# Fourteen rounding casts of a fused attention and mixture-of-experts kernel go from ScalarE to DMAs that GpSimd issues; five copies go from VectorE to ScalarE

## The chip, the cores and the metric

The kernel runs on one core of a Trainium2 chip. The metric is the device time of one execution in microseconds (us); the time shown for a kernel is the median of several runs. A profile is one further execution, recorded by the hardware profiler.

## What is computed

The reference has two parts. The first is an attention with random features, for 4 batches, 8 heads, 576 positions and 64 columns, with 128 features:

```python
def phi(x):
    proj = np.einsum('bhsd,md->bhsm', x, omega)
    sq = np.sum(x * x, axis=-1, keepdims=True) / 2.0
    h = proj - sq
    h = h - np.max(h, axis=-1, keepdims=True)
    return np.exp(h) / np.sqrt(m)
q_p, k_p = (phi(q_s), phi(k_s))
kv = np.einsum('bhsm,bhsd->bhmd', k_p, v)
z = np.sum(k_p, axis=2)
num = np.einsum('bhsm,bhmd->bhsd', q_p, kv)
den = np.einsum('bhsm,bhm->bhs', q_p, z)[..., None] + 1e-06
```

The quotient num/den is a table of 2304 tokens by 512 columns. The second part sends every token through 8 experts with weights w1 (512 by 1024) and w2 (1024 by 512), weighted by a gate matrix that is normalised 8 times over rows and columns:

```python
for e in range(E):
    h = np.maximum(x @ w1[e], 0.0)
    ye = h @ w2[e]
    out += P[:, e:e + 1] * ye
```

## The kernel before, in words

All matrix products of the experts run in float32r, a rounded form of float32. An operand is therefore split into a rounded high part (a copy with a change of type, a "cast") and a low part (operand minus high part, a "low"), and a product is made of three matmuls. On top of that the products are done by a Strassen-like scheme with seven products, numbered 1 to 7; their operands are quarters of a matrix, or sums of quarters.

Tokens come in 4 chunks of 576. A chunk's operands are made while the attention of the next tokens still runs: for chunk 0 the generator `token_operands` makes the sums on GpSimd, the casts on ScalarE (`cast`, line 120) and the lows on VectorE (line 125), and SyncE then writes each operand to DRAM. In the same way `first_splits` makes the seven operands of the first unit's w1: sums on GpSimd (line 308), casts on ScalarE (line 312), lows on VectorE (line 316). The text below calls these "token cast 2", "token low 2", "weight cast 2", "weight low 2" and so on, by the number of the product.

The attention is a software pipeline of 36 jobs (a half head group of keys or queries each). `tick(j)` issues one turn of it: projections of job j, the transposes of job j+2, the transposed copy `th` of those (line 448 on ScalarE for keys, line 450 on VectorE for queries), row maxima and shifts (lines 470 to 477, VectorE), exponentials (lines 486 and 490, ScalarE), key-value products or numerators and quotients. The sums of squares of a later job (line 415 on ScalarE, then a tree of five halving additions and two small instructions on GpSimd, lines 419 to 421) are issued near the start of a turn. I call the seven GpSimd instructions a "square set".

Twice in each turn `go_on()` takes one step of the generators above. Their steps are strings, c for a cast, l for a low, s for a sum, with one step at each bar or blank:

```python
plan = "|c1 |c3 l1.s5|c2 l3|c5 l2.s7| l5.s6|c7 |c6 l7| l6.s4| |c4 | l4|"
...
for step in "|s5.c1 | l1|c2 |c5 l2| l5.s6.s7| |c4 |c6 l4|c7 l6.s3| l7| |c3 | l3|".split():
```

So each low is issued three steps, or one and a half turns, behind its cast. Within the attention every engine executes its instructions in the order in which they were written (the list `pinned`).

Queries, keys and values come in by DMAs of SyncE; before the change GpSimd issues no DMA. After the attention, units of expert products follow until the end (lines 727 and 833, TensorE).

Of the kernel before, what the change touches and what calls it, by code (L numbers as in the profile page):

```python
# [16 lines left out]
def raw(ap):  # L17

    return ap.bitcast(F32)
# [3 lines left out]
def moe_attention_kernel(  # L23
# [23 lines left out]
    nc = tc.nc  # L47
# [51 lines left out]
    def token_tile():  # L99
        return xs.tile([P, 2, 2, HL], F32R, tag="xs", bufs=XSB, name="xs")  # L100

    def token_operands(c, x):

        def q(r, h):
            h = 1 - h
            return x[:, 2 * r : 2 * r + 2, h * HL : (h + 1) * HL]

        last = c == NCH - 1
        gate_steps = logits(c, x)
        if last:  # L110
            next(gate_steps)

        def total(o, i, s):
            eng = nc.vector if last else nc.gpsimd
            a, b = {5: (q(0, 1), s), 6: (q(1, 1), s), 7: (q(1, 1), q(0, 1)), 4: (q(1, 0), s)}[i]
            eng.tensor_tensor(o, a, b, op=ALU.subtract)

        def cast(i, o):
            t = token_tile()
            nc.scalar.copy(t[:, 0], o)  # L120
            return t

        def low(i, o, t):
            eng = nc.gpsimd if c == 1 and i in (2, 5, 7) else nc.vector
            eng.tensor_tensor(t[:, 1], o, raw(t[:, 0]), op=ALU.subtract)  # L125
            xdram[c, i] = xd.tile([P, 2, 2, HL], F32, name=f"xd{c}_{i}")
            nc.sync.dma_start(out=xdram[c, i], in_=raw(t))

        if last:
            sums = [  # L130
                sc.tile([P, H * 2 * D], F32, tag="sq", bufs=2, name="sx")[:, : 2 * HL].rearrange("p (k t) -> p k t", k=2)
                for _ in range(2)
            ]
            at = {1: q(0, 0), 5: sums[0], 6: sums[1], 3: q(1, 1), 7: q(0, 1), 2: q(1, 0), 4: sums[0]}
            tiles = {}
            for step in "c1.s5.c5.l1 s6.c6.l5 c3.l6 s7.l3.c7 l7.c2 s4.l2.c4 l4".split():
                n = len(traced)
                for what in step.split("."):
                    i = int(what[1])
                    if what[0] == "s":  # L140
                        total(at[i], i, {5: q(0, 0), 6: sums[0], 4: sums[1]}.get(i))
                    elif what[0] == "c":
                        tiles[i] = cast(i, at[i])
                    else:
                        low(i, at[i], tiles[i])
                        xop[0, c, i] = tiles[i]
                        j = i
                if j in (3, 2):
                    load_next()
                pinned.extend(traced[n:])  # L150
                first(0, c, j, 0)
                first(0, c, j, 1)
                next(gate_steps, None)
                yield
            return


        if c == 0:
            at = {i: {3: q(1, 1), 7: q(0, 1), 2: q(1, 0)}.get(i, q(0, 0)) for i in ORDER}
            plan = "|c1 |c3 l1.s5|c2 l3|c5 l2.s7| l5.s6|c7 |c6 l7| l6.s4| |c4 | l4|"  # L160
        else:
            at = {1: q(0, 0), 3: q(1, 1), 2: q(1, 0)}
            for n, i in enumerate((5, 6, 7, 4)):
                at[i] = vts[n].rearrange("p h c -> p (h c)")[:, : 2 * HL].rearrange("p (k t) -> p k t", k=2)
            plan = "|s5.c1.c3 s7.l1|s6.c2 l3.l2|w.w.c5 c7|w.l5.s4 l7.w|c6 c4|l6 l4"
        tiles = {}
        for n, step in enumerate(plan.split()):
            for part in step.split("|"):
                for what in part.split(".") if part else ():
                    if what == "w":  # L170
                        next(w2_sums)
                        continue
                    i = int(what[1])
                    if what[0] == "s":
                        total(at[i], i, {5: q(0, 0), 6: at[5], 4: at[6]}.get(i))
                    elif what[0] == "c":
                        tiles[i] = cast(i, at[i])
                    else:
                        low(i, at[i], tiles.pop(i))
                yield  # L180
            next(gate_steps, None)


    def logits(c, x):


        nt = CT // 2
        lgs = []
        for h in range(2):
            lp = bank("lp")  # L190
            for k in range(KD):
                nc.tensor.matmul(
                    lp[k * GC : (k + 1) * GC, :HL], lhsT=wgs[:, k, :], rhs=x[:, k, h * HL : (h + 1) * HL],
                    start=True, stop=True,
                )
            lg = sc.tile([P, HL], F32, tag="lg", bufs=2, name="lg")
            nc.scalar.copy(lg, lp[:, :HL])
            lgs.append(lg)
        yield
        for h, lg in enumerate(lgs):  # L200
            gp = bank("gp")
            for j in range(nt):
                nc.tensor.transpose(gp[:, j * P : (j + 1) * P], lg[:, j * P : (j + 1) * P], ident)
            t0 = c * CT + h * nt
            nc.vector.tensor_reduce(
                prob[:, t0 : t0 + nt, :],
                gp[:, : nt * P].rearrange("p (t a e) -> p t e a", a=KD, e=GC)[:, :, :E, :],
                axis=AX.X, op=ALU.add,
            )
# [81 lines left out]
    def first_splits():  # L291

        def q(r, h):
            return wst[0, 1, r][:, :, 1 - h]

        tmp[0] = wp.tile([P, 2, HD], F32, tag="t", bufs=1, name="t")
        at = {1: q(0, 0), 7: q(0, 1), 2: q(1, 0), 4: q(1, 1), 5: tmp[0], 6: tmp[0], 3: tmp[0]}
        sums = {
            5: (q(0, 1), q(1, 1), ALU.add), 6: (tmp[0], q(0, 0), ALU.subtract),
            3: (q(1, 0), tmp[0], ALU.subtract), 7: (q(0, 0), q(0, 1), ALU.subtract),  # L300
        }
        for step in "|s5.c1 | l1|c2 |c5 l2| l5.s6.s7| |c4 |c6 l4|c7 l6.s3| l7| |c3 | l3|".split():
            for part in step.split("|"):
                for what in part.split(".") if part else ():
                    i = int(what[1])
                    if what[0] == "s":
                        a, b, op = sums[i]
                        nc.gpsimd.tensor_tensor(at[i], a, b, op=op)
                    elif what[0] == "c":
                        hi = wp.tile([P, 2, HD], F32R, tag="w1h", bufs=7, name="wh")  # L310
                        lo = wp.tile([P, 2, HD], F32R, tag="w1l", bufs=7, name="wl")
                        nc.scalar.copy(hi, at[i])
                        wt[0, 1, i] = (hi, lo)
                    else:
                        hi, lo = wt[0, 1, i]
                        nc.vector.tensor_tensor(lo, at[i], raw(hi), op=ALU.subtract)
                yield
# [125 lines left out]
    def transposed_copy(jb):  # L443

        which, tp = jb[0], tps.pop(jb)
        th = sc.tile([P, 4, P], F32, tag="th", bufs=2, name="th")
        if which == "k":
            nc.scalar.copy(th.rearrange("p a s -> p (a s)"), tp)
        else:
            nc.vector.tensor_copy(th.rearrange("p a s -> p (a s)"), tp)  # L450
        ths[jb] = th
# [229 lines left out]
    def load_next():  # L681

        while loads:
            u, c, i = loads.pop(0)
            if i in RES:
                if (c, i) not in xres:
                    xres[c, i] = op_.tile([P, 2, 2, HL], F32R, name=f"xr{c}_{i}")
                    nc.sync.dma_start(out=raw(xres[c, i]), in_=xdram[c, i])
                xop[u, c, i] = xres[c, i]
                continue  # L690
            if len(early) < 2:
                xop[u, c, i] = oa[0].tile([P, 2, 2, HL], F32R, tag="oa", bufs=2, name="oa")
                early.append(i)
            else:
                xop[u, c, i] = token_tile()
            nc.sync.dma_start(out=raw(xop[u, c, i]), in_=xdram[c, i])
            return
# [237 lines left out]
    jobs = []  # L935
# [4 lines left out]
    def q_of(b):  # L940
        return [("q", (b, i // 2), i % 2, 4 * b + i // 2 * 2) for i in range(4)]
# [16 lines left out]
    jobs += mix(k_of(3), q_of(2))  # L958
    jobs += q_of(3) + [qr(0), qr(1)]

    need, seen = [], set()
    for i, jb in enumerate(jobs):
        for w in ("k", "v") if jb[0] == "k" else ("q",):
# [136 lines left out]
    xt, i, t = turned.pop(0)  # L1100
# [4 lines left out]
    xt, i, t = turned.pop(0)  # L1105
# [45 lines left out]
    for s, (u, n) in enumerate(steps):  # L1151
        c = n // (CT // 2)
# [79 lines left out]
```

## Time and profile before

| what | value |
|---|---|
| median of 3 runs | 1578.07 us (1577.44 to 1579.23) |
| the profiled execution | 1577.75 us, span 1576.0 us |
| TensorE (PE), matmuls | 1562.6 us, 99% of the span |
| VectorE (DVE) | 1363.5 us, 87% |
| ScalarE (ACT) | 766.5 us, 49% |
| GpSimd (POOL) | 277.7 us, 18% |
| the attention | from 0 to about 153 us; the experts behind it |

The span is the time from the first to the last instruction in the profile; the execution's own time is 1.75 us longer. Shares are over the whole span, and the attention, where the changed instructions stand, has other shares than the experts. TensorE's granted clock is full in every slice.

### The profile page before, as it was taken

The page shows a single profiled execution, that of the slowest core. Times are in us where ns is not written, and L with a number is a line of the kernel's source. Part 1 is how long each engine was busy: PE and PEld are TensorE (multiplying, and loading weights), DVE is VectorE, ACT ScalarE, POOL GpSimd, SP SyncE. Part 2 cuts the span into 40 slices and gives each one's busy share as a digit, 9 for nine tenths or more (in the row PEclk, how much of TensorE's full clock was granted, in tenths as well). Part 3 has the DMA queues.
Part 4 walks back from the last instruction along what each step waited for, and adds up shares of the span by engine and source line. Part 5 has one row for each costly group of instructions (what it writes and reads, how often), then busy time and mean ns, then how long its engine had stood idle before and what let it go on. Part 6 is the DMA issues. An engine that isn't in the chain of part 4 may idle for free.

```text
span 1576.0 us, 31251 instructions
## 1 busy us (share of the span) xinstructions
PE 1562.6 (99%) x12295; PEld 1537.0 (98%) x12295; DVE 1363.5 (87%) x2573; ACT 766.5 (49%) x1387; POOL 277.7 (18%) x285
## 2 busy tenths in 40 slices
PE   9999999999999999999999999999999999999999
PEld 8887999999999999999999999999999999999998
DVE  6999899989889898889888888989888888888776
ACT  8998654444444443444444444444343444444342
POOL 6665211111011111112010111111010111110000
PEclk9999999999999999999999999999999999999999
DMA  9646876656666666656566666656566655656572
GB/s 222 144 149 254 329 253 216 214 186 212 223 209 215 222 209 214 220 185 224 202 217 210 217 217 208 224 183 222 201 226 219 218 201 212 228 173 215 185 229 88
DMA packets 105730, 330.81 MB, mean 210 GB/s; under 512 B 14704, under 2 KB 43888, under 8 KB 105584
## 3 DMA queue, kind: packets, MB, share of 16 engines
q1 hardware_dynamic: 105296, 328.55, 61.8%
q8 instruction: 98, 1.61, 0.4%
q14 instruction: 48, 0.39, 0.1%
q10 hardware_dynamic: 288, 0.26, 0.0%
HBM read 307.54 MB, written 21.23 MB: 209 GB/s over the span
## 4 chain that ended last, share of the span: by engine, by line
PE 92%; DVE 5%; ACT 2%; DMA 1%; issue 0%; POOL 0%; DVEq 0%; SPq 0%; ACTq 0%; POOLq 0%
PE hx L727 25%; PE x L833 24%; PE z L833 19%; PE hz L727 19%; PE pp L460 2%; PE p L914 1%; DVE sqs L470 1%; PE kv L497 1%; PE tp L440 1%; PE np L581 1%; DMA xd<-xs 1%; DMA xs<-xd 1%; DVE xs L125 1%; PE qp L557 1%; DVE wl L267 0%
## 5 line engine op out<-in xcount | busy, mean ns | idle before, releaser
L727 PE MATMUL hx<-xs,wh 128*128 128x384 f32 x1528 | 367.1, 335 | 0.8 <-ACT hr L756 0.6
L727 PE MATMUL hz<-xs,wh 128*128 128x384 f32 x1144 | 282.5, 336 | 0.9 <-DMA xs<-xd 0.4
L727 PEld LDWEIGHTS hx<-xs,wh 128*128 128x128 f32 x1528 | 265.4, 188 | 2.1 <-ACT hr L756 0.9
L233 POOL TENSOR_TENSOR st<-st 128x512 f32<-128x512 f32 x75 | 117.3, 1564 | 620.7 <-DVE wl L267 616.3
L814 ACT ACTIVATE bh<-hr 128x512 fp32r<-128x512 f32 x141 | 89.2, 633 | 243.2 <-PE x L833 237.6
L864 DVE SCALAR_TENSOR_TENSOR out<-x,prob,out 128x256 f32<-128x256 f32 x324 | 153.9, 478 | 57.2 <-PE x L833 55.4
L727 PEld LDWEIGHTS hz<-xs,wh 128*128 128x128 f32 x1144 | 199.9, 188 | 1.8 <-DVE bl L776 0.7
L727 PE MATMUL hx<-xs,wl 128*128 128x384 f32 x764 | 199.7, 335 | 0.0
L811 DVE TENSOR_TENSOR sl<-sm,sh 128x512 fp32r<-128x512 f32 x141 | 114.5, 812 | 43.5 <-ACT sh L810 36.8
L727 PE MATMUL hz<-xs,wl 128*128 128x384 f32 x572 | 151.8, 335 | 0.0
L266 ACT CAST wh<-st 128x512 fp32r<-128x512 f32 x172 | 103.3, 620 | 99.0 <-PE hx L727 50.8
L727 PEld LDWEIGHTS hx<-xs,wl 128*128 128x128 f32 x764 | 137.3, 188 | 0.0
L810 ACT CAST sh<-sm 128x512 fp32r<-128x512 f32 x141 | 87.6, 621 | 101.7 <-PE z L833 83.0
L267 DVE TENSOR_TENSOR wl<-st,wh 128x512 fp32r<-128x512 f32 x172 | 124.0, 731 | 8.9 <-ACT wh L266 8.8
L776 DVE SCALAR_TENSOR_TENSOR sm<-hr,sm 128x256 f32<-128x256 f32 x282 | 126.5, 449 | 3.1
L797 ACT CAST sh<-sm 128x512 fp32r<-128x512 f32 x140 | 87.1, 622 | 67.7 <-PE x L833 65.5
L833 PE MATMUL z<-wh,sh 128*128 128x256 f32 x564 | 116.6, 281 | 2.1 <-ACT sh L793 1.3
L833 PE MATMUL x<-wl,sh 128*128 128x256 f32 x564 | 114.9, 280 | 0.0
L833 PE MATMUL z<-wl,sh 128*128 128x256 f32 x564 | 114.5, 280 | 0.0
L833 PE MATMUL x<-wh,sl 128*128 128x256 f32 x564 | 114.0, 279 | 0.0
L784 ACT ACTIVATE ah<-hr 128x256 fp32r<-128x256 f32 x141 | 59.0, 418 | 111.9 <-PE x L833 99.7
L833 PE MATMUL x<-wh,sh 128*128 128x256 f32 x564 | 112.8, 280 | 0.0
(192 smaller groups left out, 3556.1 us busy)
## 6 DMA issues: line engine op xcount, KB each, us to landing
xs<-xd SPq DMA_DIRECT2D x327, 768.0 KB, 4.5
st<-in_moe_w_dram SPq DMA_DIRECT2D x66, 512.0 KB, 4.8
xd<-xs SPq DMA_DIRECT2D x21, 768.0 KB, 5.3
v<-in_v_dram SPq DMA_DIRECT2D x8, 512.0 KB, 6.9
q<-in_q_dram SPq DMA_DIRECT2D x8, 512.0 KB, 7.2
k<-in_k_dram SPq DMA_DIRECT2D x7, 512.0 KB, 7.2
out_dram<-out SPq DMA_DIRECT2D x18, 128.0 KB, 4.3
oa<-xd SPq DMA_DIRECT2D x2, 768.0 KB, 8.8
```

The source lines that it names most:

```text
L233: nc.gpsimd.tensor_tensor(o, a, b, op=op)
L266: nc.scalar.copy(hi, o)
L267: nc.vector.tensor_tensor(lo, o, raw(hi), op=ALU.subtract)
L727: nc.tensor.matmul(pb, lhsT=a[:, k, g * P : (g + 1) * P], rhs=x[:, b, k, :], start=i in (1, 5, 2) and j == 0, stop=j == len(prods) - 1, sk ...
L776: nc.vector.scalar_tensor_tensor(o, in0=a, scalar=0.0, in1=b, op0=ALU.max, op1=op)
L784: nc.scalar.activation(ah, a11, AF.Relu)
L797: nc.scalar.copy(sh, sm)
L810: nc.scalar.copy(sh, sm)
L811: nc.vector.tensor_tensor(sl, sm, raw(sh), op=ALU.subtract)
L814: nc.scalar.activation(bh, a[:, 1:], AF.Relu)
L833: nc.tensor.matmul(pb, lhsT=ops[s][i][a][:, f], rhs=wt[u, 2, i][b][:, f], start=bool(start) and j == 0, stop=j == len(prods) - 1, skip_gro ...
L864: nc.vector.scalar_tensor_tensor(o, in0=pb, scalar=p, in1=o, op0=ALU.mult, op1=ALU.add)
```

## The change

The casts of chunk 0's seven token operands and of the seven operands of the first w1 are no longer ScalarE instructions. Each is a DMA from SBUF to SBUF that GpSimd issues, with a change of type on the way: 128 by 768 elements (384 KB) for a token cast, 128 by 512 (256 KB) for a weight cast. And of the queries' transposed copies, five (jobs 14, 18, 23, 27 and 30, issued in turns 12, 16, 21, 25 and 28) go from VectorE to ScalarE.

```diff
         def cast(i, o):
             t = token_tile()
-            nc.scalar.copy(t[:, 0], o)
+            if c == 0:
+                nc.gpsimd.dma_start(out=t[:, 0], in_=o)
+            else:
+                nc.scalar.copy(t[:, 0], o)
             return t
...
                         lo = wp.tile([P, 2, HD], F32R, tag="w1l", bufs=7, name="wl")
-                        nc.scalar.copy(hi, at[i])
+                        nc.gpsimd.dma_start(out=hi, in_=at[i])
                         wt[0, 1, i] = (hi, lo)
...
-        if which == "k":
+        if which == "k" or jb in on_scalar:
             nc.scalar.copy(th.rearrange("p a s -> p (a s)"), tp)
...
+    on_scalar = [jb for jb in jobs[13:32] if jb[0] == "q"][::2]
```

The change moves instructions on three engines. The first place is GpSimd around weight casts 2 and 5, about 55 to 66 us in the trace. The rows are the end of a square set (`sq`, `sqs`) and the two sums 6 and 7 of the weight operands (`t`, `st`); brackets name the semaphores that an instruction waits for. Before:

```order
L419 TENSOR_TENSOR sq<-sq 128x16x4 [waits Pool_49]
L419 TENSOR_TENSOR sq<-sq 128x16x2 [waits Pool_49]
L420 TENSOR_TENSOR sqs<-sq 128x16 [waits DVE_49,Pool_49]
L421 TENSOR_SCALAR sqs<-sqs 128x16 [waits Pool_49]
L308 TENSOR_TENSOR t<-t,st 128x512 [waits DVE_49]
L308 TENSOR_TENSOR st<-st 128x2x256
```

After, with the line numbers of the changed kernel (3 higher here):

```order
L422 TENSOR_TENSOR sq<-sq 128x16x2 [waits Pool_49]
L423 TENSOR_TENSOR sqs<-sq 128x16 [waits DVE_49,Pool_49]
L424 TENSOR_SCALAR sqs<-sqs 128x16 [waits Pool_49]
L315 DMA wh<-st 128x2x256
L315 DMA wh<-t 128x512
L311 TENSOR_TENSOR t<-t,st 128x512 [waits DMASW2_49,DVE_49]
L311 TENSOR_TENSOR st<-st 128x2x256
```

Both weight casts now stand on GpSimd behind the square set, and the sum behind them waits for a DMA too. On VectorE weight low 2 stands where it stood, but waits for the DMA of GpSimd in place of ScalarE. Before:

```order
L477 TENSOR_TENSOR ex<-pp,cn 128x512 [waits DVE_49]
L316 TENSOR_TENSOR wl<-st,wh 128x512 [waits DMAHW3_49,Activation_49]
L470 TENSOR_REDUCE sqs<-pp 128x4 [waits PE_49] x2
L475 TENSOR_REDUCE cn<-sqs 128x8 [waits DVE_49]
L477 TENSOR_TENSOR ex<-pp,cn 128x512 [waits DVE_49]
L450 COPY th<-tp 128x512 [waits PE_49]
```

After:

```order
L480 TENSOR_TENSOR ex<-pp,cn 128x512 [waits DVE_49]
L319 TENSOR_TENSOR wl<-st,wh 128x512 [waits DMAHW3_49,DMASW1_49]
L473 TENSOR_REDUCE sqs<-pp 128x4 [waits PE_49] x2
L478 TENSOR_REDUCE cn<-sqs 128x8 [waits DVE_49]
L480 TENSOR_TENSOR ex<-pp,cn 128x512 [waits DVE_49,Activation_49]
```

The row maxima of the next turn stand right behind the low, and the copy `th` of that turn is gone from VectorE.

The second place is GpSimd around weight casts 4, 6 and 7, about 70 to 79 us in the trace, from the end of one square set over the next to weight sum 3. Before:

```order
L421 TENSOR_SCALAR sqs<-sqs 128x16 [waits Pool_49]
L419 TENSOR_TENSOR sq<-sq 128x16x32 [waits Activation_49]
L419 TENSOR_TENSOR sq<-sq 128x16x16 [waits Pool_49]
L419 TENSOR_TENSOR sq<-sq 128x16x8 [waits Pool_49]
L419 TENSOR_TENSOR sq<-sq 128x16x4 [waits Pool_49]
L419 TENSOR_TENSOR sq<-sq 128x16x2 [waits Pool_49]
L420 TENSOR_TENSOR sqs<-sq 128x16 [waits Pool_49]
L421 TENSOR_SCALAR sqs<-sqs 128x16 [waits Pool_49]
L308 TENSOR_TENSOR t<-st,t 128x512 [waits DVE_49]
```

After:

```order
L424 TENSOR_SCALAR sqs<-sqs 128x16 [waits Pool_49]
L315 DMA wh<-st 128x2x256
L422 TENSOR_TENSOR sq<-sq 128x16x32 [waits Activation_49]
L422 TENSOR_TENSOR sq<-sq 128x16x16 [waits Pool_49]
L422 TENSOR_TENSOR sq<-sq 128x16x8 [waits Pool_49]
L422 TENSOR_TENSOR sq<-sq 128x16x4 [waits Pool_49]
L422 TENSOR_TENSOR sq<-sq 128x16x2 [waits Pool_49]
L423 TENSOR_TENSOR sqs<-sq 128x16 [waits Pool_49]
L424 TENSOR_SCALAR sqs<-sqs 128x16 [waits Pool_49]
L315 DMA wh<-t 128x512
L315 DMA wh<-st 128x2x256
L311 TENSOR_TENSOR t<-st,t 128x512 [waits DMASW4_49,DVE_49]
```

Weight cast 4 stands behind the first square set, casts 6 and 7 behind the second.

The third place is GpSimd from token sum 5 to token sum 7 (`xf`), about 90 to 99 us in the trace. Before:

```order
L116 TENSOR_TENSOR xf<-xf 128x2x384 [waits DVE_49,PE_49]
L419 TENSOR_TENSOR sq<-sq 128x16x32 [waits Activation_49]
L419 TENSOR_TENSOR sq<-sq 128x16x16 [waits Pool_49]
L419 TENSOR_TENSOR sq<-sq 128x16x8 [waits Pool_49]
L419 TENSOR_TENSOR sq<-sq 128x16x4 [waits Pool_49]
L419 TENSOR_TENSOR sq<-sq 128x16x2 [waits Pool_49]
L420 TENSOR_TENSOR sqs<-sq 128x16 [waits Pool_49]
L421 TENSOR_SCALAR sqs<-sqs 128x16 [waits Pool_49]
L116 TENSOR_TENSOR xf<-xf 128x2x384
```

After, where `xs` is a token operand:

```order
L116 TENSOR_TENSOR xf<-xf 128x2x384 [waits DMASW6_49,DVE_49,PE_49]
L121 DMA xs<-xf 128x2x384 [waits DMASW0_49]
L422 TENSOR_TENSOR sq<-sq 128x16x32 [waits Activation_49]
L422 TENSOR_TENSOR sq<-sq 128x16x16 [waits Pool_49]
L422 TENSOR_TENSOR sq<-sq 128x16x8 [waits Pool_49]
L422 TENSOR_TENSOR sq<-sq 128x16x4 [waits Pool_49]
L422 TENSOR_TENSOR sq<-sq 128x16x2 [waits Pool_49]
L423 TENSOR_TENSOR sqs<-sq 128x16 [waits Pool_49]
L424 TENSOR_SCALAR sqs<-sqs 128x16 [waits Pool_49]
L315 DMA wh<-t 128x512 [waits DMASW1_49]
L121 DMA xs<-xf 128x2x384
L116 TENSOR_TENSOR xf<-xf 128x2x384
```

Token cast 2 stands ahead of the square set, weight cast 3 and token cast 5 behind it. The order of the instructions on TensorE and on SyncE is the same before and after.

## Rows read from the trace of the kernel before

**Rows 1.** The chain of work that ended last: start us, us, engine, tile, line.

```profile
65.07 1.07 ACT qt L564 x2
...
70.18 0.51 ACT wh L312
...
79.23 0.72 ACT xs L120
...
85.67 0.33 DVE prob L205 x2
...
90.49 0.60 DVE th L450
...
125.45 0.69 PE np L581 x16
```

**Rows 2.** Busy time in a stretch (us): PE, PEld, DVE, ACT, POOL, clock, DMA, GB/s.

```profile
60.00:80.00 20.00, 19.76 (x336) 17.66 (x338) 18.06 (x43) 19.20 (x47) 13.83 (x24) 1.00 0.06 15
```

**Rows 3.** GpSimd's timeline, 50 to 75 us: start us, us, instruction, idle time before it.

```profile
51.22 3.68 POOL L419 TENSOR_TENSOR sq<-sq 128x512 f32<-128x512 f32 x5 [4.88 <-ACT sq L415]
...
55.51 3.34 POOL L419 TENSOR_TENSOR sq<-sq 128x512 f32<-128x512 f32 x5
...
59.24 0.64 POOL L421 TENSOR_SCALAR sqs<-sqs 128x16 f32<-128x16 f32 x1
...
64.37 1.27 POOL L308 TENSOR_TENSOR t<-t,st 128x512 f32<-128x512 f32 x1 [4.49 <-DVE wl L316]
...
69.70 3.35 POOL L419 TENSOR_TENSOR sq<-sq 128x512 f32<-128x512 f32 x5
...
74.02 3.38 POOL L419 TENSOR_TENSOR sq<-sq 128x512 f32<-128x512 f32 x5
```

**Rows 4.** VectorE's timeline: weight lows 1, 2, 5, 4 and 6.

```profile
52.25 0.79 DVE L316 TENSOR_TENSOR wl<-st,wh 128x512 fp32r<-128x512 f32 x1
...
59.07 0.68 DVE L316 TENSOR_TENSOR wl<-st,wh 128x512 fp32r<-128x512 f32 x1
...
63.60 0.68 DVE L316 TENSOR_TENSOR wl<-t,wh 128x512 fp32r<-128x512 f32 x1
...
72.96 0.68 DVE L316 TENSOR_TENSOR wl<-st,wh 128x512 fp32r<-128x512 f32 x1
...
77.59 0.68 DVE L316 TENSOR_TENSOR wl<-t,wh 128x512 fp32r<-128x512 f32 x1
```

**Rows 5.** GpSimd's timeline around token casts 2 and 7: square sets and sums.

```profile
85.00 3.95 POOL L419 TENSOR_TENSOR sq<-sq 128x512 f32<-128x512 f32 x5 [5.37 <-ACT sq L415]
...
91.34 4.98 POOL L419 TENSOR_TENSOR sq<-sq 128x512 f32<-128x512 f32 x5
...
96.93 1.82 POOL L116 TENSOR_TENSOR xf<-xf 128x768 f32<-128x768 f32 x1
99.90 1.82 POOL L116 TENSOR_TENSOR xf<-xf 128x768 f32<-128x768 f32 x1 [1.16 <-DVE rd L596]
```

**Rows 6.** VectorE's timeline: weight low 3 and token low 7.

```profile
95.41 0.81 DVE L316 TENSOR_TENSOR wl<-t,wh 128x512 fp32r<-128x512 f32 x1
...
105.93 0.95 DVE L125 TENSOR_TENSOR xs<-xf,xs 128x768 fp32r<-128x768 f32 x1
```

**Rows 7.** DMA issues: tile, queue, count, KB each, median us from issue to landing.

```profile
xd<-xs SPq DMA_DIRECT2D x21, 768.0 KB, 5.3
...
out_dram<-ol SPq DMA_DIRECT2D x12, 128.0 KB, 1.9
k<-in_k_dram SPq DMA_DIRECT2D x2, 256.0 KB, 3.3
```

**Rows 8.** SyncE's DMA issues of token operands: duration of the issue, ns min/median/max.

```profile
L127 SPq DMA_DIRECT2D xd<-xs x21: 319/320/680, 87.2 to 162.1; - x21
...
L696 SPq DMA_DIRECT2D xs<-xd x1: 901/901/901, 162.9 to 162.9; - x1
```

**Rows 9.** Waits in 65 to 125.4 us: waiting row, releaser, us, times, longest.

```profile
DVE sqs L470 <- PE pp L460: 1.4, 4, 0.5
```

## The prediction

> **What bounds the kernel now.** I read the busy shares first: TensorE has 99% of the span, so only the stretch in which other engines hold it up can move, and that is the attention. The chain of waits, read through the attention, puts the end on TensorE up to 65.07 us, on ScalarE from there to about 85.7, on VectorE from 85.67 to 125.45, and then on TensorE again [rows 1]. No engine is far behind another: in 60 to 80 us TensorE, VectorE and ScalarE are busy for 19.8, 18.1 and 19.2 of 20 us, GpSimd for 13.8, and the DMA engines hardly (0.06) [rows 2]. So a few tenths taken from one engine are soon lost at the next, while a wait of several us on VectorE is paid by all: the query and key pipeline has six PSUM banks, and a turn's projections need the banks that VectorE's shifts and ScalarE's exponentials give back.
>
> Then I followed GpSimd and the lows on VectorE side by side, since each of the fourteen casts becomes an instruction that waits its turn on GpSimd, and a low on VectorE waits for it in order.
>
> **What is removed.** ScalarE loses 14 casts; in the chain a weight cast is worth 0.51 us and a token cast 0.72 [rows 1]. VectorE loses five copies of 0.60 us in the chain [rows 1], 4 of them in turns behind 59 us: 2.4 us. ScalarE gains five such copies. On the ScalarE-bound stretch 65 to 85 us this takes away three weight casts and two token casts, 3 x 0.51 + 2 x 0.72 = 3.0 us, and adds one copy, some 0.5 (an estimate, by a weight cast of the same 128 by 512): 2.5 us net.
>
> **What is added.** Call p the time for which GpSimd is held by the issue of one cast DMA, and D the time from the moment at which GpSimd reaches it to the moment at which its data has landed and the low may start. No row of before shows either.
> - D: from below the shortest landing of the trace, 1.9 us for 128 KB; from above the 5.3 us of a 768 KB write of token operands. A weight cast moves 256 KB, so I take the 256 KB row, 3.3 us [rows 7]. A token cast moves 384 KB; between 3.3 and 5.3 I take 4.3.
> - p: SyncE's issues of token operands take 0.32 us (median) and 0.90 us [rows 8]. GpSimd takes 1.27 us for a sum of the size for which VectorE takes 0.68 [rows 3, 4], so I take the slower of the two, 0.9; the upper bound is one of its token sums, 1.82 [rows 5].
>
> The Trainium skill (DMA: Bandwidth & Descriptors, section "Anatomy of one DMA — SWDGE (gpsimd) path") gives about 2.0 us fixed plus the bytes at 436 GB/s; for 256 KB that is an estimate of 2.6 us. With 2.6 for D the sum below would be 8 us in place of 10. No run of before shows such a DMA.
>
> **Where each cast lands.** The low is three half turns behind its cast, which was enough while ScalarE made it. On GpSimd the square sets stand ahead.
> - Weight cast 1: GpSimd is idle for 4.88 us before 51.22, so it goes out at 46.3 and lands at 49.6 (51.6 with 5.3); low 1 runs at 52.25 [rows 3, 4]. No wait.
> - Weight casts 2 and 5: two square sets run back to back from 51.22 to 59.24 + 0.64 = 59.88 [rows 3], and both casts stand behind the second. Cast 2 lands at 59.88 + 3.3 = 63.2; VectorE stands at low 2 at 59.07 [rows 4]. Wait: 4.1 us. Behind low 2 in VectorE's order are the maxima and shifts of the next turn, so ScalarE's exponentials and then TensorE's projections stop as well. Cast 5 lands 0.9 later, in time for low 5, which was 4.5 us behind low 2 (63.60).
> - Weight cast 4: sum 6 on GpSimd follows low 5 (it starts at 64.37 when low 5 ends); then come sum 7, a small and a full square set, up to 74.02 [rows 3]. This row of work hangs on low 5 and moves with it. So cast 4 lands at 74.02 + 3.3 = 77.3, against low 4 at 72.96 [rows 4], both plus the earlier wait: 4.4 us more.
> - Weight casts 6 and 7: one more set of 74.02 - 69.70 = 4.32 us lies ahead [rows 3]. Cast 6 lands at 74.02 + 0.9 + 4.32 + 3.3 = 82.5; low 6, at 77.59 [rows 4] plus 4.4, is at 82.0. Wait: 0.6. Cast 7 is covered by this.
> - Token casts 1 and 3 go out behind weight sum 3 in a stretch where GpSimd is idle for 5.37 us [rows 5]. No wait.
> - Weight cast 3: a square set (85.00), token sum 5, token cast 2 and another set, until 96.93 [rows 5] plus p of cast 2, then 3.3: 101.1, against low 3 at 95.41 [rows 6]. That is 5.7. But the first of these sets starts at 85.00 because ScalarE is late with its squares; relieved by 2.5 us it may be up to that much earlier. I take half: 4.5 us. Token low 2 stands right ahead of low 3 and its wait is part of this.
> - Token cast 7: GpSimd makes sum 6 from 99.90 to 101.72 after low 5, then issues cast 7, which lands at 106.0 against low 7 at 105.93 [rows 5, 6]. Next to nothing; with 5.3 it would be 1.1. Casts 6 and 4 of the tokens are alike and looser.
>
> Sum of waits: 4.1 + 4.4 + 0.6 + 4.5 = 13.6 us. Against it stand VectorE's 2.4 us of copies and the 1.4 us for which it waited for projections in 65 to 125.4 us [rows 9], since a VectorE that is late no longer waits there: 3.8. Net +9.8 us. Nothing behind takes it back: after 125.45 the chain is on TensorE [rows 1], and the experts keep it 99% busy to the end. Against the profiled execution, 1577.75 + 9.8 = **1587.5 us** (the median shown is 0.3 us above that execution).
>
> **The bounds.** With D = 1.9 and p = 0.32, and the whole 2.5 us of relief: 2.7 + 3.0 + 0.0 + 1.2 = 6.9, less 3.8 is +3.1: 1580.9. With D = 5.3, p = 1.82 and no relief: 6.1 + 6.4 + 1.5 + 8.6 + 1.1 = 23.7, less 3.8 is +19.9: 1597.7.
>
> **The rivals.**
> - *The waits are swallowed (about the same).* Up to 65.07 the chain is TensorE's, so VectorE's first wait costs only what TensorE can't run ahead. If half of the first wait is lost that way (2 us), and D is near its floor, the net is +1: about 1579. For it: GpSimd's queue was idle 5 us here and there [rows 3, 5]. Against it: VectorE is busy for 18 of 20 us in that stretch and can't catch up 4 us, and the second and third waits hang on GpSimd's own row of work, which moves along.
> - *Faster: the relief of ScalarE is what counts.* Its place is 65 to 85 us, its price 2.5 us there, and 2 x 0.60 us of copies in turns 25 and 28 on VectorE behind it: 1577.75 - 3.7 = 1574. It decides only if GpSimd is at weight cast 2 by 59.07 - 3.3 = 55.8 us, and at cast 4 by 69.7. The rows say 59.88 and 74.02 [rows 3, 4]: even a landing in no time would be 0.8 and 1.1 us late, so the relief would have to outweigh that.
> - *Dearer DMAs.* The cast DMAs take as long as the large writes, or GpSimd is held up by VectorE while it makes them: 1593 to 1598 by the upper bound. For it: the square set at 91.34 took 4.98 us for what took 3.35 at 69.70 [rows 3, 5], so GpSimd does lose time while lows run on VectorE. Against it: at the first two waits VectorE stands still while the DMA is being made.
>
> The Trainium skill (SBUF — State Buffer, section "Who interferes with whom") has GpSimd share SBUF ports with VectorE, with one blocking the other, and warns of DMAs from GpSimd that wait for their descriptors. It speaks against this change and for the dearer case; the 4.98 us row agrees with the sharing, and nothing before shows a DMA held up by it. By it I would add 1.6 us (4.98 - 3.35) to the third wait: 1589.
>
> **How the numbers follow.** A measurement of this kernel tells about 0.2% (3.2 us) from no change. The waits as worked out, between 1581 and 1592: 0.64. Dearer DMAs, 1592 and above: 0.15. Swallowed, within 3.2 us: 0.13. Faster by more: 0.08. So slower 0.79, same 0.13, faster 0.08. The likeliest case gives 1587.5. The range for 8 in 10 reaches down into the swallowed waits and up to near the upper bound: 1579.5 to 1597.
>
> **What the changed profile would show.** Right: VectorE's waits put weight lows 2, 4 and 3 down to DMAs of `wh`, 3 to 6 us each, TensorE's slices before 130 us fall below those of before, `wh` and `xs` DMAs appear on a GpSimd queue with 2 to 5 us to landing, and the first product of the experts starts some 10 us later than before. The first step that can fail is D: under 1.5 us the net is near zero. The second is GpSimd's lag: if its square sets end 4 us earlier against the lows, the waits are gone and the faster case is left. The third is how far TensorE runs ahead. If the attention is no longer than before, the argument on square sets is wrong; if it is longer but the lows don't wait for DMAs, the cause is another.

## The result, and the profile after

The changed kernel takes 1594.42 us (median; 1592.33 to 1595.52) against 1578.05 us for the kernel before in the same comparison: ratio 1.0103, 95% interval 1.009 to 1.0115. It is slower, by 16.4 us. The forecast was 1587.5 with a range of 1579.5 to 1597, and 0.79 for slower.

The profiled execution of the changed kernel took 1592.33 us, its span is 1590.5, that is 14.5 us more than before. The line numbers are up to 5 higher than before. First the place at which the loss ends: VectorE's row maximum over the gates, which follows the attention (start us, us, instruction). Before:

```profile
154.68 0.29 DVE L636 TENSOR_REDUCE m<-prob 128x1 f32<-128x144 f32 x1
```

After:

```profile
168.36 0.29 DVE L639 TENSOR_REDUCE m<-prob 128x1 f32<-128x144 f32 x1
```

So 13.7 of the 14.5 us are lost inside the attention. Next the weight lows on VectorE's timeline after (numbers 1, 2, 4, 6 and 3; brackets: idle time before the instruction and what ended it), the rows that answer to [rows 4, 6]:

```profile
53.39 0.94 DVE L319 TENSOR_TENSOR wl<-st,wh 128x512 fp32r<-128x512 f32 x1 [0.84 <-DMA wh<-st]
...
63.84 0.69 DVE L319 TENSOR_TENSOR wl<-st,wh 128x512 fp32r<-128x512 f32 x1 [3.41 <-DMA wh<-st]
...
80.53 0.83 DVE L319 TENSOR_TENSOR wl<-st,wh 128x512 fp32r<-128x512 f32 x1 [3.49 <-DMA wh<-st]
...
85.71 0.69 DVE L319 TENSOR_TENSOR wl<-t,wh 128x512 fp32r<-128x512 f32 x1 [0.98 <-DMA wh<-t]
...
109.31 0.69 DVE L319 TENSOR_TENSOR wl<-t,wh 128x512 fp32r<-128x512 f32 x1 [7.28 <-DMA wh<-t]
```

Five of seven weight lows wait for their DMA, 16.0 us in all; before, none waited [rows 4, 6]. The same on GpSimd's timeline, for casts 2, 5, 4, 6 and 3 and the token cast behind the last (start us, us, instruction):

```profile
55.47 3.31 POOL L422 TENSOR_TENSOR sq<-sq 128x512 f32<-128x512 f32 x5
...
59.36 0.79 POOL L315 DMA_DIRECT2D wh<-st  x1
60.15 0.56 POOL L315 DMA_DIRECT2D wh<-t  x1
68.59 1.27 POOL L311 TENSOR_TENSOR t<-t,st 128x512 f32<-128x512 f32 x1 [7.88 <-DVE wl L319]
...
77.87 0.80 POOL L315 DMA_DIRECT2D wh<-st  x1
...
82.98 0.62 POOL L315 DMA_DIRECT2D wh<-t  x1
...
98.58 3.95 POOL L422 TENSOR_TENSOR sq<-sq 128x512 f32<-128x512 f32 x5
...
103.14 0.62 POOL L315 DMA_DIRECT2D wh<-t  x1
103.76 0.71 POOL L121 DMA_DIRECT2D xs<-xf  x1
```

Casts 2, 4, 6 and 3 each stand behind a square set, as the order showed (the sets ahead of 4 and 6 are left out here). The row of sum 6 shows the loop that the waits make: it waits 7.88 us for low 5 on VectorE, which had itself been held by low 2's DMA, and the next square sets and casts stand behind it.

Both timelines together give two numbers for each wait. VectorE was ready for low 2 at 63.84 - 3.41 = 60.43; GpSimd had reached cast 2 at 59.36. So 1.1 us were left for the DMA, and it needed 63.84 - 59.36 = 4.5; that is D of the prediction.

| weight low | left from cast to low, us | D, us | waited, us |
|---|---|---|---|
| 2 | 1.1 | 4.5 | 3.4 |
| 4 | -0.8 | 2.7 | 3.5 |
| 6 | 1.7 | 2.7 | 1.0 |
| 3 | -1.1 | 6.2 | 7.3 |

A minus says that VectorE stood at the low before GpSimd had come to the cast. The chain of waits now goes through GpSimd and the DMAs (start us, us, what), where before it was on ScalarE and VectorE [rows 1]; its last row here is token cast 5, issued right behind weight cast 3 and landed 0.9 us after it:

```profile
59.36 4.46 DMA wh<-st
63.84 0.69 DVE wl L319
...
68.59 1.27 POOL t L311
...
82.98 2.63 DMA wh<-t
85.71 0.69 DVE wl L319
...
103.76 6.47 DMA xs<-xf
```

And the stretches of 20 us (busy us of PE, PEld, DVE, ACT, POOL, then clock, DMA share, GB/s; the DMA share adds up the time that packets took, and can exceed 1), the first answering to [rows 2]:

```profile
60.00:80.00 20.00, 17.82 (x296) 15.97 (x296) 12.78 (x30) 16.26 (x40) 11.11 (x20) 1.00 0.24 58
100.00:120.00 20.00, 13.58 (x207) 11.82 (x207) 11.35 (x24) 10.92 (x29) 12.02 (x19) 0.83 0.83 228
```

TensorE lost 1.9 us in the first and is busy for 13.6 of 20 in the second, in which its granted clock also falls to 0.83.

### The profile page after: what moved, and what is told of

The parts are those of the page before. It is cut to its first block, busy times and chain, and to the rows that moved or that the text cites. A ratio compares the mean times of both kernels' runs of the same rounds, so it can differ in the third digit from the quotient of the medians.

```text
span 1590.5 us, 31278 instructions
## 1 busy us (share of the span) xinstructions
PE 1564.2 (98%) x12295; PEld 1538.1 (97%) x12295; DVE 1359.6 (85%) x2568; ACT 761.5 (48%) x1378; POOL 288.1 (18%) x299
## 4 chain that ended last, share of the span: by engine, by line
PE 89%; DMA 3%; DVE 3%; POOL 2%; ACT 2%; issue 1%; SPq 0%; DVEq 0%; POOLq 0%; ACTq 0%
PE hx L730 24%; PE x L836 24%; PE z L836 18%; PE hz L730 18%; POOL sq L422 1%; DMA xs<-xd 1%; PE p L917 1%; PE pp L463 1%; DMA k<-in_k_dram 1%; DMA xs<-xf 1%; PE np L584 0%; PE qp L560 0%; DVE wl L270 0%; DVE sqs L473 0%; DVE out L867 0%
```

## The experiments

Ratios are to the kernel before in the same comparison, whose median was 1577.8 to 1578.3 us. The last column is VectorE's idle time ahead of the fourteen lows whose casts the change moves, where it waits for the cast. The diffs show the lines that matter; plan strings are shown alone.

| kernel | us | ratio to before, 95% | waits for casts, us |
|---|---|---|---|
| the change | 1594.42 | 1.009 to 1.0115 | 16.0 |
| five copies alone | 1578.41 | 0.9993 to 1.001 | none |
| weight casts alone | 1596.58 | 1.0102 to 1.013 | 16.0 |
| token casts alone | 1582.50 | 1.0017 to 1.0039 | 4.2 |
| GpSimd copies, no DMA | 1581.88 | 1.0014 to 1.0032 | 4.9 |
| DMAs issued by ScalarE | 1579.38 | 1.0 to 1.0018 | 3.1 |
| plain DMAs on GpSimd | 1594.52 | 1.009 to 1.0117 | 17.0 |
| square sets at the turn's end | 1595.23 | 1.0095 to 1.0123 | 15.3 |
| weight low 3 late | 1593.58 | 1.0079 to 1.011 | 15.1 |
| weight lows late | 1583.21 | 1.002 to 1.0045 | 4.3 |
| all lows late | 1583.11 | 1.0019 to 1.0043 | 1.1 |
| weight casts alone, lows late | 1579.42 | 1.0001 to 1.0019 | none |
| TensorE kept busy | 1592.56 | 1.0079 to 1.0107 | 16.4 |

**The three parts.** My theory: the waits of the weight lows are the cost, the copies a small credit. A rival: the three parts add up to something else, above all through the token casts. First the copies alone, all casts staying on ScalarE; against the kernel before:

```diff
-        if which == "k":
+        if which == "k" or jb in on_scalar:
...
+    on_scalar = [jb for jb in jobs[13:32] if jb[0] == "q"][::2]
```

> Only the five copies of queries go to ScalarE; all casts stay ScalarE instructions as before. Theory (the loss is VectorE standing at weight lows 2, 4, 6 and 3 for DMAs that GpSimd issues late): none of the loss is here, 1575.5 to 1578.5 us, no wait of VectorE for a DMA of wh. Rival 'ScalarE is overloaded by the copies' would give more than 1583.

They change nothing that can be measured. Then the weight casts alone; this diff and the later ones, but for the next, are against the changed kernel:

```diff
-            if c == 0:
-                nc.gpsimd.dma_start(out=t[:, 0], in_=o)
-            else:
-                nc.scalar.copy(t[:, 0], o)
+            nc.scalar.copy(t[:, 0], o)
...
-        if which == "k" or jb in on_scalar:
+        if which == "k":
```

> Only the seven weight casts are DMAs of GpSimd; token casts and copies as before. Theory: nearly the whole loss is here. Waits at lows 1, 2, 4 and 6 as in the changed kernel (about 0.8, 3.4, 3.5, 1.0 us), at low 3 less than the 7.3 us (3.5 to 5), since token cast 5 is no DMA behind it: 12 to 14 us of waits, 1586 to 1592 us. If the wait at low 3 stays under the length at which TensorE's clock fell, the granted clock of 100 to 120 us is 1.00. Rival 'the token DMAs are the cost': under 1582.

The waits in 40 to 170 us (releaser, us in all, times, longest):

```profile
DVE wl L316 <- DMA wh<-st: 8.2, 3, 5.1
DVE wl L316 <- DMA wh<-t: 7.8, 2, 6.7
```

This half alone has the whole loss, and more: 4.6 us above the upper end of what I expected. The expected relief at low 3 did not come: it waits 6.7 us without any token cast beside it. And the token casts alone, against the kernel before:

```diff
-            nc.scalar.copy(t[:, 0], o)
+            if c == 0:
+                nc.gpsimd.dma_start(out=t[:, 0], in_=o)
+            else:
+                nc.scalar.copy(t[:, 0], o)
```

> Only the seven token casts of chunk 0 are DMAs of GpSimd; weight casts and copies as before. Theory: no low waits for a DMA, 1574 to 1579 us. Rival 'traffic': 2.7 MB more through the DMA engines delay SyncE's writes of token operands and with them the first expert products, over 1583 us, with waits of ScalarE or VectorE for xd or xs.

One low waits, token low 5, whose cast GpSimd had come to at 95.30:

```profile
101.52 0.96 DVE L128 TENSOR_TENSOR xs<-xf,xs 128x768 fp32r<-128x768 f32 x1 [4.19 <-DMA xs<-xf]
```

The kernel is 4.7 us above before, against my expectation of none. In the whole change this wait is hidden, since VectorE is held at weight low 3 then. The parts don't add: 16.4 us for the whole, 18.8 and 4.7 for the halves.

**GpSimd's order or the landing?** Two kernels take these apart. In the first the casts stay where they are on GpSimd, but as its own copies (the line of the token casts changes in the same way, here and in the next two kernels):

```diff
-                        nc.gpsimd.dma_start(out=hi, in_=at[i])
+                        nc.gpsimd.tensor_copy(hi, at[i])
```

> The whole change, but each of the fourteen casts is a copy instruction of GpSimd in the place of its DMA: the same place in line behind the square sets, without a transfer to land. Theory (a wait is GpSimd's lag plus the landing, and the landing is the larger part): a copy takes about 1 us (256 KB) to 1.5 us (384 KB), so low 2 hardly waits, low 4 about 2 us, low 3 about 2, token low 5 little: 3 to 6 us of waits in all, no fall of the granted clock, 1577 to 1583 us. Rival 'the place in line alone costs it': the waits stay above 10 us and the time above 1588.

```profile
DVE wl L319 <- POOL wh L315: 4.9, 3, 2.3
```

So GpSimd's lag, with a copy of 0.6 us behind it, makes the lows wait 4.9 us. In the second ScalarE issues the DMAs at the places of its former casts:

```diff
-                        nc.gpsimd.dma_start(out=hi, in_=at[i])
+                        nc.scalar.dma_start(out=raw(hi), in_=at[i])
```

> The fourteen DMAs are issued by ScalarE in place of GpSimd, at the places of its former casts, as plain copies without a change of type. It leaves out the rounding: the high part is the whole value and the low part zero; sizes, lows, writes and everything else are those of the changed kernel. My theory (5 us are GpSimd's lag, the rest is the landing beside other DMAs): without GpSimd's queue lows 2, 4 and 6 no longer wait or wait below 1 us, while low 3 and the token lows behind 100 us still wait 2 to 5 us for DMAs that land in 4 to 8 us; 1580 to 1588. Rival A (it is the lag behind the square sets alone): no wait for a DMA above 1 us, 1576 to 1579. Rival B (the copy from SBUF to SBUF is dear whoever issues it): waits as in the changed kernel, 14 us and more, 1592 or above.

```profile
47.91 0.68 ACTq L315 DMA_DIRECT2D wh<-st  x1
...
56.74 0.60 ACTq L315 DMA_DIRECT2D wh<-st  x1
...
91.29 0.50 ACTq L315 DMA_DIRECT2D wh<-t  x1
```

```profile
54.27 0.69 DVE L319 TENSOR_TENSOR wl<-st,wh 128x512 fp32r<-128x512 f32 x1 [2.09 <-DMA wh<-st]
62.11 0.69 DVE L319 TENSOR_TENSOR wl<-st,wh 128x512 fp32r<-128x512 f32 x1 [1.02 <-DMA wh<-st]
...
96.69 0.81 DVE L319 TENSOR_TENSOR wl<-t,wh 128x512 fp32r<-128x512 f32 x1
```

The first fence has casts 1, 2 and 3 on ScalarE's queue, the second the lows. None of the fourteen lows waits behind 100 us, and the kernel is within 0.2% of before: I had counted the landing as a cost of its own, and that was wrong. The first of these DMAs are not quick: low 1 runs 6.4 us behind its cast, low 2 5.4. But ScalarE reaches the cast early: cast 2 has 62.11 - 1.02 - 56.74 = 4.4 us until VectorE is ready, cast 3 has 5.4, where on GpSimd 1.1 and -1.1 were left. GpSimd's lag with its own copies costs 4.9 us of waits, the DMAs without that lag 3.1, the two together 16.0: each alone fits nearly into the one and a half turns between cast and low, and both don't. At cast 3 there is more to it. Issued by ScalarE at 91.29, it landed after 2.9 us (the DMA engines' share was 0.56 and 0.40 in the two windows of 2 us from 90); issued by GpSimd at 103.14 it took 6.2, beside a share of 0.9 to 1.15. So this kernel does not price that landing by itself: the place in the order also chose the traffic which the DMA met.

That the DMA changes the type on the way could have made it slow. The same DMAs on GpSimd without that:

```diff
-                        nc.gpsimd.dma_start(out=hi, in_=at[i])
+                        nc.gpsimd.dma_start(out=raw(hi), in_=at[i])
```

> The changed kernel with its fourteen DMAs still issued by GpSimd at the same places, but as plain copies without a change of type. It leaves out the rounding: the high part is the whole value and the low part zero. My theory (the landing is the transfer beside other DMAs, the change of type has no part in it): waits 14 to 17 us, issue 0.5 to 0.9 us each, 1592 to 1597, as the changed kernel. Rival (the change of type makes the DMA slow): landings of 256 KB nearer the 3.3 us of the loads, waits below 11 us, 1589 or below.

The time is that of the changed kernel, the waits nearly so (17.0 us, of which low 3 has 7.33). The change of type has no part in it that these runs can tell.

**More room, or the same room elsewhere.** Here the square sets are issued at the end of the turn in place of near its start so that casts no longer stand behind them in the same half turn:

```diff
             maxima(now, 0)
-        if j >= 3:
-            ensure_squares(j)
...
             go_on()
+        if j >= 3:
+            ensure_squares(j)
```

> The whole change, with the fourteen DMAs as they are, but each turn's square set is issued at the end of the turn, so that on GpSimd a cast DMA stands ahead of that turn's square set. Theory: weight casts 2, 4 and 6 go out about 4.3 us earlier against their lows, so lows 2, 4, 6 wait 0 to 2 us in place of 3.4, 3.5 and 1.0, low 3 about 3 in place of 7.3, token low 5 up to 4: 4 to 8 us of waits in all, 1579 to 1586 us. Rival 'GpSimd's line is no matter, the DMA takes as long as it takes': as the changed kernel, 1592 us or more.

It missed: lows 2, 4 and 6 wait 0.3, 1.8 and 0.2 us, but low 1 now 4.2, low 7 2.0 and low 3 6.8. GpSimd has the same work for the same time, and other casts stand behind it. Moving low 3 alone by a turn went the same way (the ends of the two strings):

```diff
-l7| |c3 | l3|
+l7| |c3 | | | l3|
```

> The whole change, with weight low 3 alone two steps (one turn) later. My theory (each low that finds its DMA not landed is paid by all, and the idle TensorE behind low 3 loses clock on top): low 3 no longer waits, the waits of lows 1, 2, 4 and 6 stay at 8 to 9 us, TensorE's granted clock stays at 0.95 or above in 100 to 120 us, token low 5 waits 2 to 4 us in place of low 3, as it did where the weight lows were late; 1594.4 - 7.3 - 2.3 + 3 = 1588, between 1586 and 1590. Rival (the wait comes back at the next low in full, as with the square sets at the end of the turn): waits still 15 us or more, 1592 or above.

The rival was right. Low 3 no longer waits, and token low 5, the next to need a late DMA, does:

```profile
113.01 0.96 DVE L128 TENSOR_TENSOR xs<-xf,xs 128x768 fp32r<-128x768 f32 x1 [6.12 <-DMA xs<-xf]
117.26 1.13 DVE L319 TENSOR_TENSOR wl<-t,wh 128x512 fp32r<-128x512 f32 x1
```

So the whole weight plan: casts as early as their sums allow, lows further behind them.

```diff
-"|s5.c1 | l1|c2 |c5 l2| l5.s6.s7| |c4 |c6 l4|c7 l6.s3| l7| |c3 | l3|"
+"|s5.c1.c2.c4.c5 | |l1 l2| l5|s6.s7.c6.c7 |l4 | | l6|s3.c3 |l7 | | l3|"
```

> The whole change, with the same fourteen DMAs and five copies, but weight casts 1, 2, 4 and 5 go out in one step at the start and every weight low comes about seven steps (three and a half turns) behind its cast. Theory (what costs is that the lows come too early for GpSimd's place in line plus the landing): waits of VectorE for DMAs under 2 us in all, granted clock 1.00 throughout, 1573 to 1578 us, 16 to 20 us under the changed kernel. Rival 'the DMAs themselves cost, wherever the lows stand' (traffic, ports of GpSimd and VectorE): over 1585 us.

Eleven us of the sixteen come back, where I had expected all: no weight low waits, and what is left is token low 5 again (4.27 us). With token casts on ScalarE and copies on VectorE, this plan shows what the weight half is worth without its waits:

> The seven weight casts alone by DMA, with the weight plan in which they are issued early and their lows stand further behind; token casts on ScalarE and the five copies on VectorE as before. My theory (a cast on GpSimd costs nothing where the slack to its low exceeds the sum of GpSimd's lag and the landing): no weight low waits more than 1 us, no token low can wait for a DMA, and the kernel is level with before, 1576 to 1580. Relief that counts: ScalarE is quicker in 65 to 85 us and the kernel is faster than before, 1574 to 1576. Rival (the DMAs cost time beyond the waits on them, by GpSimd's hold at the issue and the later plan): 1581 or above, as with all lows late.

Casts 1, 2 and 4 are issued on GpSimd in one go, and low 2 runs without a wait some 11 us later:

```profile
45.70 2.36 POOL L312 DMA_DIRECT2D wh<-st  x3
```

```profile
57.48 0.68 DVE L316 TENSOR_TENSOR wl<-st,wh 128x512 fp32r<-128x512 f32 x1
```

1579.42 against 1577.90: 17.3 of the 18.8 us of the weight half are gone with the waits, and no gain stands behind it, though ScalarE makes seven casts fewer. The same late plan with casts on ScalarE was not run, so what the order of the lows is worth by itself is not known. For the tokens the same was tried (more room for the token lows too):

```diff
-"|c1 |c3 l1.s5|c2 l3|c5 l2.s7| l5.s6|c7 |c6 l7| l6.s4| |c4 | l4|"
+"|c1 c3|c2 |l1.s5.s7 c5|l3 l2|c7 | l5.s6|c6 l7| | l6.s4|c4 | | l4|"
```

> As the experiment with late weight lows, and the token lows too come five to six steps behind their casts (weight lows seven), with token sum 7 made earlier. That experiment left one wait, 4.3 us of token low 5, and a fall of the granted clock behind it. Theory: both go away; waits of VectorE for DMAs under 1 us, granted clock 1.00, 1574 to 1579 us. Rival 'the DMAs cost by their traffic or by GpSimd's time': it stays at 1582 or above.

It missed: the lows wait 1.1 us in all, and still it is 1583.11. The chain of waits is on GpSimd there from 84.8 to 98.7 us, with a square set, two token sums of 1.8 us and another set in a row, and then on a token cast:

```profile
98.66 7.89 DMA xs<-xf
```

The three kernels with token casts on GpSimd's DMAs and without weight waits are thus 4.7 to 5.4 us above before, with waits of 1.1 to 4.3 us, and the granted clock of 100 to 120 us is 0.83 to 0.95 in all three. Which part of this a better order could save stays open.

**The clock.** Since low 3's wait leaves TensorE idle and its clock falls behind that, I gave it something to do: the projections of turn 25 are made five times over (the values are the same).

```diff
-    def projections(jb):
+    def projections(jb, times=1):
...
-            projections(now)
+            projections(now, 5 if j == 25 else 1)
```

> The whole change, but in turn 25 TensorE makes the projections five times instead of once (the same values into the same banks, 4 x 1.09 us of extra work), which fills most of the 6.4 us in which it stood idle while VectorE waited for weight cast 3. Theory (that idle stretch lets the granted clock fall to its lower level, and the slow matmuls behind it cost about 2 us on top of the wait): the granted clock stays 1.00 behind it, and the time falls by 1 to 3 us against the changed kernel, to 1591 to 1594. Rival 'the fall of the clock is hidden behind VectorE': no change, or up to 1 us slower by the extra work.

1592.56 against the 1594.42 of the change, but the two ratios' intervals overlap. The idle time shrank from 6.4 to 2.9 us and the clock of 100 to 120 us rose from 0.83 to 0.91; it fell all the same. Nor are the two profiles alike elsewhere: in 60 to 80 us, behind low 2, the clock is 0.83 here and 1.00 in the profile of the change. What the clock costs in the whole stays open, 1.9 us being what the medians say.

## Why the prediction was right, and where its sizes were off

**The direction, and its cause, hold.** Lows 2, 4, 6 and 3 wait for DMAs that GpSimd issues behind its square sets, token low 7 does not, and the experts give nothing back. Take the weight casts off GpSimd's DMAs, and 4.7 us or less of the 16.4 are left; give the weight lows more room, and of the 18.8 us of the weight half 1.5 are left.

**The waits: 13.6 foretold, 16.0 measured.** By lows 1, 2, 4, 6 and 3: 0, 4.1, 4.4, 0.6 and 4.5 foretold; 0.8, 3.4, 3.5, 1.0 and 7.3 measured. What failed is D, which I took as 3.3 us for every weight cast. It was 2.7 at casts 4 and 6, 4.5 at cast 2 and 6.2 at cast 3. The lag was well sized at low 3, for which I had GpSimd 1.2 us behind VectorE, and it was 1.1: its 2.8 us too many are D. At low 2 the near hit is luck: I had GpSimd 0.8 us behind, it was 1.1 ahead, and a D that was 1.2 too small made up for most of that. Low 1 waited at all because of D too: its cast was reached at 46.5, and the low ran 6.9 us later. D goes with what else the DMA engines carry, by the windows of 2 us after (columns as above):

```profile
60.00:62.00 2.00, 2.00 (x24) 1.82 (x22) 0.43 (x1) 2.00 (x7) 0.71 (x2) 1.00 1.35 310
...
82.00:84.00 2.00, 0.39 (x6) 0.39 (x8) 1.79 (x7) 1.14 (x5) 1.75 (x6) 1.00 0.01 4
...
104.00:106.00 2.00, 1.85 (x43) 1.59 (x38) 0.00 (x0) 0.00 (x0) 1.99 (x2) 1.00 1.12 382
```

Cast 2 (59.36) went into loads of values and queries, cast 3 (103.14) into a load of queries and a write of a token operand, cast 6 (82.98) into idle DMA engines. That is read from rows, and no run changes that traffic alone. In the kernel with weight casts alone the stretch from 104 to 110 us is as full (1.0 to 1.1), and cast 3 took 5.6 us there to land; from ScalarE, in a quieter stretch, it took 2.9. The rows that could have told me were in the view from which I took D: I held to the 3.3 us of a load of 256 KB, with the 5.3 of the large writes as the upper bound [rows 7], and passed over loads of half that size:

```profile
kr<-in_k_dram SPq DMA_DIRECT2D x4, 128.0 KB, 6.6
vr<-in_v_dram SPq DMA_DIRECT2D x4, 128.0 KB, 6.9
```

So size did not order the landings even before, and my upper bound was below landings of the same trace; two of the five (6.9 and 6.2 us) lie above it.

The Trainium skill (DMA: Bandwidth & Descriptors, section "Issuing engines are not separate DMA queues") has the DMAs of all issuing engines interleave on the same 16 DMA engines, with which these rows agree. It adds that starting DMAs on several engines at once saves only the sequencer's time at the issue, usually little beside the transfer. Here more than that hung on the engine that issues: 1579.38 us with plain DMAs from ScalarE and 1594.52 with them from GpSimd, since each DMA goes out when its engine's order comes to it.

The Trainium skill (DMA: Bandwidth & Descriptors, section "Anatomy of one DMA — SWDGE (gpsimd) path") would give an estimate of 2.6 us for 256 KB. The two casts in quiet stretches agree, with 2.7 us; the others took up to 6.9.

**The issue, p: 0.9 foretold, 0.56 to 0.93 measured** for weight casts. Right, and of little weight. The dearer case's second cause, that VectorE holds up GpSimd while it makes a DMA, has no row for it: cast 2 took 0.79 us on GpSimd and cast 4 0.80, beside VectorE busy or idle.

**The credits: 3.8 foretold, 2.3 obtained.** The attention ended 13.7 us later with 16.0 us of waits. The copies, 2.4 of my 3.8, are worth nothing by themselves (ratio 1.0002), nor are seven casts fewer on ScalarE (the late weight plan). Where three engines are busy for 18 to 20 of 20 us [rows 2], an instruction taken from one of them moved nothing; I said so of the path, and then booked the copies as a gain. Beside the waits it may be otherwise: the weight casts alone cost 18.8 us and the whole change 16.4. But the two intervals overlap, the clock in 60 to 80 us differs between the two profiles (0.83 and 1.00), and no run has weight casts and copies without token casts, so from where the 2.3 us come stays open.

**The sum.** Against the forecast of +9.8 for the profiled execution: 2.4 more of waits, 1.5 less of credits, 0.8 behind the attention (span 14.5 against 13.7) and 0.1 outside the span make 14.6, which is 1592.33 - 1577.75. The median is 2.1 us above that execution. The other three executions had a mean clock of 0.995 to 0.996, the profiled one 0.998; a fall of the clock was no term of my sum. A second fall would fit, such as the one in 60 to 80 us with the weight casts alone, but those three executions left no profile.

**The rivals.** Swallowed and faster fell with the waits and with the copies' zero. The case of dearer DMAs, 1593 to 1598, is where the time came out, to which I had given 0.15, against 0.64 for the waits as worked out. Its first half holds for two of the five casts that were waited for (6.9 and 6.2 us, against 5.3 for the large writes); for its second half there is no row.

## What to carry to other kernels

For each operand that moves to a DMA, work out from the timelines the time between the moment at which the issuing engine reaches it and the moment at which its reader is ready; that room, less the landing in that very stretch, decides, and a lag and a landing that each cost little can be dear together. Moving work to an engine with idle time costs its order: GpSimd was idle for a third of the stretch, and still came late to its casts, because a set of some 4 us stood ahead. And taking copies from an engine that was busy for nine tenths beside two others as busy gained nothing here by itself.

## What the runs showed of the hardware

TensorE's granted clock fell after a wait of another engine. After, TensorE was idle from 105.85 to 112.27 us and then ran at half clock, 0.50 or 1.2 GHz, up to about 117:

```profile
108.00:110.00 2.00, 0.00 (x0) 0.00 (x0) 0.69 (x2) 0.00 (x0) 0.00 (x0) 1.00 0.30 78
110.00:112.00 2.00, 0.00 (x0) 0.00 (x0) 1.86 (x5) 0.49 (x2) 0.00 (x0) 0.56 0.00 0
...
114.00:116.00 2.00, 2.00 (x14) 1.64 (x14) 1.86 (x5) 1.52 (x4) 1.98 (x3) 0.50 1.08 362
116.00:118.00 2.00, 2.00 (x26) 1.61 (x26) 1.26 (x3) 1.82 (x6) 1.84 (x3) 0.73 1.25 219
```

```profile
104.69 1.16 PE L463 MATMUL pp<-omt,th 64*128 64x128 f32 x16
112.27 1.12 PE L443 MATMUL tp<-ident,k 128*128 128x128 f32 x4 [6.42 <-DVE ex L480]
113.18 1.97 PE L560 MATMUL qp<-ident,ex 128*128 128x128 f32 x8
115.08 2.08 PE L463 MATMUL pp<-omt,th 64*128 64x128 f32 x16
```

Sixteen projections take 2.08 us there and 1.16 at full clock. In the kernel with projections made five times over, TensorE was idle for 2.9 us at this place, and eight of the products `qp` still took 2.10 us behind it. Not every idle stretch did this: behind the wait at low 2 of the changed kernel TensorE was idle for 2.18 us, and the clock stayed at 1.00 from 66 to 72 us; with the weight casts alone it was idle for 4.38 us at that place, and then ran at 0.50 from 68 to 74.
